# The last output tile in column parts of 384 and 128 instead of 256 and 256

## The chip, the core and the metric

The kernel runs on one core of a Trainium2 chip. The metric is device time in microseconds (us); the times below are from three timed runs and from one profiled execution. The engines are named as in the profile: PE is TensorE's matmuls, PEld its weight loads (which overlap the matmuls), DVE is VectorE, ACT is ScalarE, POOL is GpSimd, SP is SyncE, which issues the DMAs.

## The reference

Two attentions in a row, then a gated feed-forward layer:

```
p_packed = sm_attn(p, k, v)              # batch 8, heads 8, sequence 576, head 64; 32 packed queries
out = sm_attn(q, p_packed, p_packed)
x = out.transpose(0, 2, 1, 3).reshape(4608, 512)
a = x @ w_a                              # 512 x 1536
b = x @ w_b                              # 512 x 1536
result = (a * b) @ w_out                 # 1536 x 512, float32
```

## The kernel before, in words

The kernel walks over the 8 batches. For each it computes `h = a * b`, transposed, in 12 tiles of 128 rows of the hidden dimension (`NFT` is 12): `mm1` makes one of them in two matmul groups of 288 columns each (lines 356 to 381). Between these groups a written plan (`PLAN`, `emit`) places the attention steps of the next batch. Then the second product, `mm2_part` (line 387), makes the output for 128 tokens at a time: the 128x128 tile of `h` is the stationary operand and `w_out` streams past it.

To keep float32 accuracy every operand of the large products is split in a high and a low word (`_hi`, `_lo`, both of type float32r, kept as `h_hi`, `h_lo`, `wo_hi`, `wo_lo`), and a product is three matmuls: high with high, high with low, low with high. One output tile of 128 tokens therefore takes 12 x 3 = 36 matmuls, each with a weight load of its own of 128x128. Usually each streams all 512 columns of the output (`DO` is 512), and one ScalarE copy and one store follow (`mm2_out`).

The last tile of the last batch (`last`) is done differently. It is made in two column parts, one after the other, each in a PSUM buffer of its own from the pool `ps_m` (in the profile it is called `m`). ScalarE copies the first part to the output tile `ob` (in the profile `asb`), VectorE the second part; each part has a store of its own from SP's queue (line 403). So the copy and the store of the first part can run while TensorE works on the second part. After the second part nothing is left for TensorE, and what follows it is the program's tail: a VectorE copy, a DMA issue, the transfer, and the end.

Plain float32 matmuls, with operands that were not split, appear elsewhere in the kernel; `warm` (line 534), which streams 512 columns of a loaded tile nine times past the identity matrix, is one, and the transposes of lines 147 to 152 and 271 to 272 also stream float32 past the identity, by `nc.tensor.transpose`.

Of the kernel before, what the change touches and what calls it, by code (L numbers as in the profile page):

```python
# [19 lines left out]
def tile_packed_attn_gated_ffn(  # L20
# [20 lines left out]
    nc = tc.nc  # L41
# [3 lines left out]
    DO = out.shape[1]  # L45
    P = 128
# [44 lines left out]
    def bank_pair(s=False):  # L91
        return ps_s.tile([P, 2, 512], F32, name="s") if s else ps_m.tile([P, 2, 512], F32, name="m")
# [291 lines left out]
    def mm2_part(o, c0, fts, cols=slice(0, DO)):  # L384
        for ft in fts:
            for n, (ht, wt) in enumerate(((h_hi[ft], wo_hi[ft]), (h_hi[ft], wo_lo[ft]), (h_lo[ft], wo_hi[ft]))):
                nc.tensor.matmul(  # L387
                    out=o[:, cols], lhsT=ht[:, c0:c0 + P], rhs=wt[:, cols],
                    start=(ft == 0 and n == 0), stop=(ft == NFT - 1 and n == 2))

    def store(b, ob, c0, cols=slice(0, DO)):

        if b == 0:
            for i in range(2):
                store_first(ob, c0 // 64 + i, 64 * i)
            return
        t0 = b * S - 64 * (b % 2) + c0
        parts = [(t0 + 64 - S, 0, 64), (t0 + 64, 64, 64)] if c0 < 64 * (b % 2) else [(t0, 0, P)]
        if b == 1 and c0 == 0:
            store_first(ob, 0, 0)  # L400
            parts = parts[1:]
        for t, i, n in parts:
            nc.sync.dma_start(out=out[t:t + n, cols], in_=ob[i:i + n, cols])
# [10 lines left out]
    def out_tile(i):  # L414

        if i % 3 == 1:
            return sm.tile([P, DO], F32, name="wo_f32", bufs=1)
        return sm.tile([P, 2, HS], F32, name="asb").rearrange("p u t -> p (u t)")[:, 0:DO]
# [124 lines left out]
    for name in FIRST.split():  # L543
        what, i = name[0], int(name[1])
# [58 lines left out]
            mm2_out(b, o, c0, i)  # L603

    ob = out_tile(0)
    for i in range(2):
        o = bank_pair()[:, 0, :]
        cols = slice(i * DO // 2, (i + 1) * DO // 2)
        mm2_part(o, last, range(NFT), cols)
        copy = nc.vector.tensor_copy if i else nc.scalar.copy  # L610
        copy(out=ob[:, cols], in_=o[:, cols])
        store(B - 1, ob, last, cols)

# [29 lines left out]
```

## Time and profile before

| | |
|---|---|
| three timed runs, median (lowest, highest) | 732.89 us (731.39, 733.14) |
| profiled execution, its own time | 733.02 us |
| its span, first to last instruction | 731.2 us |
| TensorE matmul busy in the span | 98% |
| TensorE weight loads busy | 84% |
| VectorE, ScalarE, GpSimd busy | 41%, 39%, 29% |
| granted TensorE clock | mean 1.000 of full; 0.9 or more in all 40 slices |

The span is 1.8 us shorter than the profiled execution's time; what lies around it is not in the trace. A busy share says how long an engine had something in flight. Matmuls are pipelined, so a matmul's own duration is longer than the step from one to the next; what a matmul costs in a row of them is that step.

### The profile page before, as it was taken

How to read it: one execution, taken by the hardware profiler on the slowest of the kernel's cores; microseconds unless marked ns; L12 is line 12 of the kernel's file. 1: busy time of each engine (PE TensorE's matmuls, PEld its weight loads, DVE VectorE, ACT ScalarE, POOL GpSimd, SP SyncE). 2: the span in 40 equal slices, each digit the busy share in tenths (PEclk: the TensorE clock that was granted, in tenths of full speed). 3: DMA queues.
4: the chain of work that ended last, by engine and by line, in shares of the span. 5: the costliest groups of instructions: out<-in, count | busy, mean ns of one | idle time of the engine just before them, and what ended most of it. 6: DMA issues, size and time to landing. Idle time of an engine off the chain costs nothing.

```text
span 731.2 us, 14205 instructions
## 1 busy us (share of the span) xinstructions
PE 717.2 (98%) x6086; PEld 615.1 (84%) x6086; DVE 302.7 (41%) x487; ACT 281.7 (39%) x495; POOL 211.9 (29%) x154
## 2 busy tenths in 40 slices
PE   5899999999999999999999999999999999999998
PEld 4488878898888988898888988889888898898987
DVE  2788655456204562245602456045620546024100
ACT  2788743543115431354204442154311543135200
POOL 0486752334003340133202342033400334023300
PEclk9999999999999999999999999999999999999999
DMA  8999964350501505033320333215050100000011
GB/s 233 387 253 306 247 120 80 68 108 8 108 30 32 99 9 107 16 66 72 61 62 16 66 72 68 56 34 99 1 109 30 34 1 16 30 15 1 1 33 41
DMA packets 171007, 58.34 MB, mean 80 GB/s; under 512 B 140608, under 2 KB 158784, under 8 KB 170944
## 3 DMA queue, kind: packets, MB, share of 16 engines
q1 hardware_dynamic: 170944, 57.43, 32.2%
q8 instruction: 48, 0.79, 0.5%
q14 instruction: 15, 0.12, 0.0%
HBM read 47.97 MB, written 9.44 MB: 79 GB/s over the span
## 4 chain that ended last, share of the span: by engine, by line
PE 93%; DMA 3%; SPq 1%; ACT 1%; DVE 1%; issue 0%; DVEq 0%
PE m L361 42%; PE m L387 41%; PE x L343 4%; DMA raw<-in_moe_w_b_dram 2%; PE s L281 2%; PE m L343 1%; PE s L247 1%; DMA qn<-in_q_dram 1%; PE s L271 1%; PE s L297 1%; DVE w_ab L200 0%; PE x L236 0%; PE s L343 0%; PE m L297 0%; SPq L177 0%; SPq L169 0%
## 5 line engine op out<-in xcount | busy, mean ns | idle before, releaser
L387 PE MATMUL m<-wo,h_hi 128*128 128x512 f32 (+1 forms) x888 | 268.8, 385 | 0.0
L86 POOL TENSOR_TENSOR h_lo<-asb,h_hi 128x576 fp32r<-128x576 f32 x96 | 138.1, 1439 | 399.9 <-ACT h_hi L380 399.6
L376 DVE TENSOR_TENSOR asb<-m,asb 128x576 f32<-128x576 f32 x96 | 72.7, 757 | 307.0 <-PE m L361 302.3
L387 PEld LDWEIGHTS m<-wo,h_hi 128*128 128x128 f32 x888 | 164.2, 188 | 36.0 <-issue 3.4
L361 PE MATMUL m<-a_hi,ghi 128*128 128x288 f32 x768 | 169.5, 302 | 1.6 <-ACT ghi L349 1.5
L387 PE MATMUL m<-wo,h_lo 128*128 128x512 f32 (+1 forms) x444 | 170.2, 383 | 0.0
L361 PE MATMUL m<-a_lo,ghi 128*128 128x288 f32 x768 | 163.8, 295 | 0.3 <-DVE a_lo L86 0.3
L361 PEld LDWEIGHTS m<-a_hi,ghi 128*128 128x128 f32 x768 | 122.5, 188 | 20.7 <-issue 5.0
L361 PE MATMUL m<-a_hi,glo 128*128 128x288 f32 x768 | 133.7, 296 | 0.0
L361 PEld LDWEIGHTS m<-a_lo,ghi 128*128 128x128 f32 x768 | 123.9, 189 | 0.5 <-DVE a_lo L86 0.5
L380 ACT CAST h_hi<-asb 128x576 fp32r<-128x576 f32 x96 | 64.6, 673 | 143.5 <-DVE asb L376 143.5
L361 PEld LDWEIGHTS m<-a_hi,glo 128*128 128x128 f32 x768 | 112.9, 188 | 0.2 <-DVE glo L86 0.2
L387 PEld LDWEIGHTS m<-wo,h_lo 128*128 128x128 f32 x444 | 83.5, 188 | 16.5
L373 ACT COPY asb<-m 128x576 f32<-128x576 f32 x96 | 61.6, 642 | 30.9 <-PE m L361 24.0
L422 ACT COPY asb<-m 128x512 f32<-128x512 f32 x24 | 14.1, 587 | 133.3 <-PE m L387 132.2
L86 DVE TENSOR_TENSOR glo<-x,ghi 128x512 fp32r<-128x512 f32 x68 | 43.6, 682 | 4.5 <-ACT ghi L349 3.9
L343 PE MATMUL x<-w_ab,ppT 64*32 64x512 f32 x544 | 38.8, 591 | 0.2 <-DVE w_ab L200 0.2
L349 ACT CAST ghi<-x 128x512 fp32r<-128x512 f32 x68 | 36.6, 591 | 5.8 <-PE x L343 5.2
L119 DVE STREAM_TRANSPOSE xT<-nat 128x1152 f32<-128x1152 f32 x28 | 38.3, 1369 | 0.6 <-DMA nat<-in_k_dram 0.6
L422 ACT COPY wo_f<-m 128x512 f32<-128x512 f32 x11 | 6.5, 588 | 53.8 <-PE m L387 53.8
L189 ACT ACTIVATE raw<-raw 128x512 f32<-128x512 f32 x36 | 23.1, 681 | 1.9 <-DMA raw<-in_moe_w_a_dram 1.8
L315 POOL TENSOR_TENSOR t<-t,sum 128x576 f32<-128x576 f32 x14 | 16.5, 1179 | 24.9 <-DVE sum L314 24.9
(116 smaller groups left out, 474.3 us busy)
## 6 DMA issues: line engine op xcount, KB each, us to landing
nat<-in_k_dram SPq DMA_DIRECT2D x56, 144.0 KB
nat<-in_q_dram SPq DMA_DIRECT2D x56, 144.0 KB
vt<-in_v_dram SPq DMA_DIRECT2D x28, 256.0 KB
raw<-in_moe_w_a_dram SPq DMA_DIRECT2D x12, 512.0 KB
raw<-in_moe_w_b_dram SPq DMA_DIRECT2D x12, 512.0 KB
raw<-in_moe_w_out_dram SPq DMA_DIRECT2D x12, 512.0 KB
out_dram<-asb SPq DMA_DIRECT2D x17, 256.0 KB
out_dram<-wo_f SPq DMA_DIRECT2D x10, 256.0 KB
```

The source lines that it names most:

```text
L86: return eng.tensor_tensor(out=dst, in0=src, in1=hi.bitcast(F32), op=ALU.subtract)
L119: nc.vector.transpose(out=xT.rearrange("p h t -> p (h t)"), in_=t.rearrange("p h x d -> p (h x d)"))
L189: nc.scalar.activation(out=high, in_=high, func=AF.Prelu, scale=2.0 ** -112, alpha=-2.0 ** 32)
L315: eng.tensor_tensor(out=s2, in0=s2, in1=sum2.unsqueeze(2).broadcast_to([P, TU, J]), op=ALU.mult)
L343: nc.tensor.matmul(out=gps[e][J * r:J * r + J, 0:2 * P * n], lhsT=ppT[rows, 2 * (b % 2), r, :], rhs=w if n == 2 else w[:, fts[0] % 2], sta ...
L349: nc.scalar.copy(out=hi, in_=part)
L361: nc.tensor.matmul(out=ps[:, half, 0:HS], lhsT=gt[:, kt, ft % 4, cols], rhs=at[:, kt, HS * half:HS * half + HS], start=(n == 0 and kt == 0 ...
L373: nc.scalar.copy(out=asb, in_=pa[:, :, 0:HS])
L376: nc.vector.tensor_tensor(out=asb, in0=pb[:, :, 0:HS], in1=asb, op=ALU.mult)
L380: nc.scalar.copy(out=hh, in_=flat)
L387: nc.tensor.matmul(out=o[:, cols], lhsT=ht[:, c0:c0 + P], rhs=wt[:, cols], start=(ft == 0 and n == 0), stop=(ft == NFT - 1 and n == 2))
L422: nc.scalar.copy(out=ob, in_=o)
```

## The change

The two parts of the last tile are no longer 256 columns each. The first part has 384 columns, still copied by ScalarE; the second has 128, still copied by VectorE. The number of matmuls (36 in each part), their weight loads, their order, the copies and the stores are the same in number.

```diff
     ob = out_tile(0)
-    for i in range(2):
+    for cols, copy in ((slice(0, DO - P), nc.scalar.copy), (slice(DO - P, DO), nc.vector.tensor_copy)):
         o = bank_pair()[:, 0, :]
-        cols = slice(i * DO // 2, (i + 1) * DO // 2)
         mm2_part(o, last, range(NFT), cols)
-        copy = nc.vector.tensor_copy if i else nc.scalar.copy
         copy(out=ob[:, cols], in_=o[:, cols])
         store(B - 1, ob, last, cols)
```

On TensorE, where the first part of the last tile ends and the second begins, the order before is this (`m` is the PSUM buffer, `wo` the split `w_out`, `h_hi` and `h_lo` the split hidden tiles; the shape is what a matmul writes):

```order
L387 MATMUL m<-wo,h_lo_507 128x256
L387 MATMUL m<-wo,h_hi_508 128x256 x2
L387 MATMUL m<-wo,h_lo_509 128x256
L387 MATMUL m<-wo,h_hi_486 128x256 x2
L387 MATMUL m<-wo,h_lo_487 128x256
```

In the same place now:

```order
L387 MATMUL m<-wo,h_lo_507 128x384
L387 MATMUL m<-wo,h_hi_508 128x384 x2
L387 MATMUL m<-wo,h_lo_509 128x384
L387 MATMUL m<-wo,h_hi_486 128x128 x2
L387 MATMUL m<-wo,h_lo_487 128x128
```

No matmul moved: the same tiles follow one another, wider up to the middle and narrower from there. The end of SP's queue, which issues the stores, before (-) and now (+):

```order
 L403 DMA out_dram<-wo_f_7146 128x512
 L403 DMA out_dram<-asb 128x512 x2
-L403 DMA out_dram<-asb 128x256 x2
-L638 UNCONDITIONAL_BRANCH
+L403 DMA out_dram<-asb 128x384
+L403 DMA out_dram<-asb 128x128
+L636 UNCONDITIONAL_BRANCH
```

The two stores stand where they stood, with other widths.

## Rows read from the trace of the kernel before

**Rows 1.** The page: span, busy times, then the chain that ended last, by engine

```profile
span 731.2 us, 14205 instructions
PE 717.2 (98%) x6086; PEld 615.1 (84%) x6086; DVE 302.7 (41%) x487; ACT 281.7 (39%) x495; POOL 211.9 (29%) x154
PE 93%; DMA 3%; SPq 1%; ACT 1%; DVE 1%; issue 0%; DVEq 0%
```

**Rows 2.** The chain over 719 to 731.2 us: start, length, what

```profile
718.95 9.10 PE m L387 x74
728.04 0.04 DVEq L611
728.08 0.04 issue
728.12 0.42 DVE asb L611
```

**Rows 3.** Timeline of matmuls at L387: start, us until the last one's end

```profile
686.58 0.63 PE L387 MATMUL m<-wo,h_hi 128*128 128x512 f32 x2
...
719.24 0.40 PE L387 MATMUL m<-wo,h_hi 128*128 128x256 f32 x2
...
723.55 0.40 PE L387 MATMUL m<-wo,h_hi 128*128 128x256 f32 x2
...
727.75 0.28 PE L387 MATMUL m<-wo,h_lo 128*128 128x256 f32 x1
```

**Rows 4.** Groups by line and shape, 686.5 to 731.2 us: busy, mean ns

```profile
L387 PE MATMUL m<-wo,h_hi 128*128 128x512 f32 x96 | 29.6, 389 | 0.0
...
L387 PE MATMUL m<-wo,h_hi 128*128 128x256 f32 x48 | 8.7, 283 | 0.0
```

**Rows 5.** Four matmuls of 288 columns at 686 us: timeline, then their group

```profile
686.04 0.69 PE L361 MATMUL m<-a_hi,glo 128*128 128x288 f32 x4
L361 PE MATMUL m<-a_hi,glo 128*128 128x288 f32 x2 | 0.4, 293 | 0.0
```

**Rows 6.** Timeline at 723 us, a weight load and its matmul

```profile
723.31 0.19 PEld L387 LDWEIGHTS m<-wo,h_lo 128*128 128x128 f32 x1
723.43 0.28 PE L387 MATMUL m<-wo,h_lo 128*128 128x256 f32 x1
```

**Rows 7.** Weight loads of the whole span, by line and shape

```profile
L387 PEld LDWEIGHTS m<-wo,h_hi 128*128 128x128 f32 x888 | 164.2, 188 | 36.0 <-issue 3.4 <-ACT a_hi L319 0.4
...
L343 PEld LDWEIGHTS x<-w_ab,ppT 64*32 64x32 f32 x544 | 12.2, 106 | 4.6 <-PE m L534 1.0 <-issue 1.0 <-DVE w_ab L200 0.4
...
L271 PEld LDWEIGHTS s<-ident,t 128*128 128x128 f32 x56 | 6.9, 141 | 0.0
...
L272 PEld LDWEIGHTS s<-ident,t 128*64 128x64 f32 x14 | 1.6, 111 | 0.0
```

**Rows 8.** Transposes of L152: timeline of loads and matmuls, then the line's durations

```profile
21.56 0.57 PEld L152 LDWEIGHTS x<-ident,qn 32*128 32x128 f32 x8 [0.17 <-issue]
21.56 0.68 PE L152 MATMUL x<-ident,qn 32*128 32x32 f32 x8
L152 PEld LDWEIGHTS x<-ident,qn x8: 133/137/138, 21.6 to 22.0; 32*128 32x128 f32 x8
L152 PE MATMUL x<-ident,qn x8: 220/222/243, 21.6 to 22.0; 32*128 32x32 f32 x8
```

**Rows 9.** Plain float32 at L534: the line's count, then twelve in the timeline

```profile
L534 PE MATMUL m<-kn,ident x18: 592/592/697, 25.0 to 32.4; 128*128 128x512 f32 x18
27.64 5.31 PE L534 MATMUL m<-kn,ident 128*128 128x512 f32 x12
```

**Rows 10.** Copies: both parts of the last tile, and wider ones of either engine

```profile
L611 DVE COPY asb<-m 128x256 f32<-128x256 f32 x1 | 0.4, 425 | 40.5 <-PE m L387 40.5
L611 ACT COPY asb<-m 128x256 f32<-128x256 f32 x1 | 0.4, 373 | 3.7 <-PE m L387 3.7
L422 ACT COPY asb<-m 128x512 f32<-128x512 f32 x3 | 1.8, 588 | 21.8 <-PE m L387 21.8
L376 DVE TENSOR_TENSOR asb<-m,asb 128x576 f32<-128x576 f32 x1 | 0.8, 758 | 2.4 <-PE m L361 2.4
```

**Rows 11.** The last store: its issue, then DMA in 40 slices of 728 to 731.2 us

```profile
728.57 0.33 SPq L403 DMA_DIRECT2D out_dram<-asb  x1
DMA  0000000000000000028999510000000000000000
GB/s 0 0 0 0 0 0 0 0 0 0 0 0 0 0 0 0 0 90 294 346 358 333 192 26 0 0 0 0 0 0 0 0 0 0 0 0 0 0 0 0
```

**Rows 12.** The two halves and the tail, as windows: width, busy, PEclk, DMA, GB/s

```profile
719.24:723.55 4.31, 4.31 (x37) 4.31 (x36) 1.00 0.16 61
723.55:727.87 4.32, 4.32 (x38) 4.27 (x36) 1.00 0.11 34
727.87:731.20 3.33, 0.16 (x2) 0.00 (x0) 1.00 0.12 39
```

## The prediction

> **What bounds the kernel now.** I read the page first. Matmuls fill 98% of the span, and 93% of the chain that ended last is TensorE [rows 1]. So time is what TensorE's rows take, plus what follows the last of them. Then I took the chain over the last 12 us, to see who sets the end there: TensorE on line 387 without a break until 728.04 us, then the VectorE copy of the second part, 0.42 us [rows 2]. After it come the issue of the store, the transfer, and the end at 731.2 us. The first part's copy and store stand nowhere in this chain; they run under the second part. So two things count: the steps of 72 matmuls, and the tail behind the last one.
>
> Next the step from one matmul to the next, which is not the duration of one. 144 matmuls of 512 columns start between 686.58 and 719.24 us: 32.66 / 144 = 226.8 ns each. The 72 of 256 columns start from 719.24 to 727.75: 8.51 / 71 = 119.9 ns each [rows 3]. The difference over 256 more columns is 106.9 ns, or 0.418 ns a column, which is 2.4 GHz (the granted clock is 1.00 in these windows [rows 12]); about 13 ns do not depend on the width. The 288-column matmuls fit on the line: four take 0.69 us and one lasts about 0.29, so (0.69 - 0.29) / 3 = 133 ns [rows 5], and the line gives 119.9 + 32 x 0.418 = 133. Down to 256 columns, then, the columns alone set the step. The trace has no float32r matmul narrower than that.
>
> **The first part, 256 to 384 columns.** The line gives 119.9 + 128 x 0.418 = 173.3 ns a step. 36 of them: 36 x (173.3 - 119.9) = 1.92 us more. This term is an interpolation between measured widths, and I trust it to 0.1 us.
>
> **The second part, 256 to 128 columns.** If columns alone set the step here too, it is 119.9 - 53.5 = 66.4 ns, and what the first part loses comes back. The question is whether the weight loads let it. Each matmul has a 128x128 load of its own. At 256 columns the load for a matmul starts at 723.31 and its matmul at 723.43 [rows 6], about one step later, so a load has 120 ns and needs no more than that; with 66 ns it may need more than it has. The loads' durations (188 ns) contain a delay that overlaps with other loads, or a 120 ns step would not be possible. I take the delay out by comparing widths. A plain float32 load of 32 columns takes 106 ns, the 128-column load of line 387 takes 188: 82 / 96 = 0.854 ns a column, or 109 ns for 128 columns. The loads of the transposes are cheaper: 111 ns at 64 columns, 141 at 128 [rows 7], 0.469 ns a column, so 60 ns for 128.
>
> The second figure can be tried. The transposes of line 152 load 128 columns each and stream only 32, so that little but the load can set their step: eight loads in 0.57 us with 0.137 for the last make (0.57 - 0.137) / 7 = 62 ns, the matmuls (0.68 - 0.222) / 7 = 65 ns [rows 8]. The slope gave 60, so it forecasts a step bound by loads to 2 to 5 ns. For the loads of line 387 that makes 109 + 3 = **112 ns**, and I take it for the 128-column step. It is bounded by 66.4 ns below (columns alone) and 119.9 above, where loads of this very shape are seen to keep up.
>
> From the first start to the last there are 36 steps of the first part and 35 of the second, then the last matmul itself. That one lasts 283 ns at 256 columns and 389 at 512 [rows 4], so about 230 at 128. Before: 8.51 + 0.28 = 8.79 us. After: 36 x 173.3 + 35 x 112 + 230 = 6.24 + 3.92 + 0.23 = 10.39 us. TensorE loses **1.60 us**. By the bounds: 8.79 us at 66.4 ns (nothing lost), 10.67 at 119.9 (1.87 lost).
>
> Here a rule speaks against me. The Trainium skill, "TensorE: Matmul & The Clock Gate", section "Back-to-back issue gap", gives about 81 ns for a matmul of 128 columns in a sustained row of loads and matmuls. By its 81 ns the second part would be 35 x 31 = 1.1 us shorter than mine, and TensorE would lose an estimated 0.5 us. The same sentence has 131 ns for 512 columns, where this trace shows 227, so here the measured step decides for the wide matmul, and no run shows the narrow one yet.
>
> **The tail.** The last copy has half the columns. VectorE's copy of 256 takes 425 ns; between it and the 576-column pass of the same engine lies 333 ns for 320 columns, 1.04 ns each [rows 10]. 128 fewer save 0.13 us. The last store carries 64 KB instead of 128. Before, its data move in seven slices of 0.08 us, at most 0.56 us, from 729.36; its issue stood at 728.57 [rows 11]. The 0.8 us ahead of the data and the 1.3 us behind it are a wait that I leave as it is. Half of 0.56 is 0.28, if the transfer goes by bytes; if it goes by rows (128 in both cases) the gain is nothing. I take 0.2, since the rate near the middle of the transfer is flat, which is how bytes would look. Tail: **-0.33 us** (bounds -0.13 to -0.41).
>
> **What costs nothing.** ScalarE's first copy grows by 128 columns at (588 - 373) / 256 = 0.84 ns [rows 10], 0.11 us, and its store by 64 KB. Both lie under the second part, which at 112 ns a step is 36 x 112 = 4.0 us long. Copy (0.48 us), issue (0.33) and the 1.35 us from the issue to the end of the data that the last store shows [rows 11] make some 2.2 us, so they fit even under a part of 36 x 66.4 = 2.4 us. If that cover were gone, the price would be the rest of the first transfer ahead of the second, at most 0.3 us.
>
> **The sum.** 1.60 - 0.33 = +1.27 us on the profiled execution's 733.02 us (a span of 731.2 and 1.8 around it): 734.3. The median of the runs is 0.13 lower, so **734.2 us**, 0.17% slower. About 0.3%, 2.2 us, is what a measurement of this kernel can tell from no change, so this counts as the same.
>
> **The rivals.**
> - *The columns alone set the narrow step.* The loads are hidden at 66.4 ns as they are at 120; then TensorE loses nothing and the tail gains: 732.89 - 0.33 = 732.6 us. For it speaks the clean line from 512 down to 256; against it the slope of the load durations. By the 81 ns of the Trainium skill ("TensorE: Matmul & The Clock Gate", the section above) the time would lie between this and my sum, at an estimated 733.1 us.
> - *Narrow float32r goes at plain float32's pace.* The trace has float32r at 0.42 ns a column, but only at 256 and wider. Plain float32 is far slower: the nine matmuls of line 534 stand as 18 in the trace, each (5.31 - 0.592) / 11 = 429 ns after the one before [rows 9]. That is 858 ns for 512 columns, or 214.5 for 128. If the fast pace fails below some width, 35 x (214.5 - 112) = 3.6 us come on top of my sum, and it is 737.8 us: slower, by 0.7%. This decides from a step of about 140 ns on, where the sum passes 2.2 us. For it: every float32r matmul of the trace is at least 256 wide, so nothing contradicts it. Against it: plain float32 shows two loads and two matmuls for each, and no reason is seen why a narrower shape would add instructions.
> - *The loads do not get below 120 ns.* A variant of my case: 1.87 - 0.33, 734.4 us.
>
> **How the numbers follow.** I give 0.56 to the load-bound step (with the variant), 0.18 to the columns alone, 0.21 to the slow pace, 0.05 to anything else. The likeliest case by itself, with the bounds of its terms and the 1.75 us that the three runs are apart, is 733.2 to 735.2 us. Stopping there or at 732 below would leave the slow pace's 0.21 and more outside, so the range goes from 731.9 to 738.2. Slower by over 0.3%: the slow pace (0.21), a load-bound case that the scatter carries over 735.1 (0.05), something else (0.02): 0.28. Faster by over 0.3% needs under 730.7, which no case reaches without scatter: 0.03. The same: 0.69.
>
> **What would show it.** In the profile after: first-part matmuls 173 ns apart; second-part ones 112 ns apart, with a load busy throughout the second part, and a second part 4.0 us long instead of 4.3. The last copy would take 0.29 us, and from its end to the end of the span 2.5 us instead of 2.7. A second part of 2.4 us means the columns decide and I am wrong on the loads; one of 7 us or more means the slow pace. A first part that is not 6.2 us long would break the line itself.

## The result and the profile after

The changed kernel takes 734.14 us (median of 19 runs, 732.95 to 735.51), the kernel before 732.76 (19 runs, 731.39 to 733.74). The ratio is 1.0019, with a 95% interval from 1.0012 to 1.0025: slower by 0.9 to 1.8 us, 1.4 by the medians. That is a real loss, and within the 0.3% that I had called no change.

The profiled spans are 731.2 and 732.0 us, only 0.8 apart. Spans of single executions aren't the measure here: the last tile began at 719.24 us before and at 718.69 after, and the work ahead of it is the same in both. What the change did is read from that start on. Before, it is 731.2 - 719.24 = 11.96 us [rows 2, 3]; after, 732.0 - 718.69 = 13.31, that is **1.35 us more** (spans are given to 0.1 us), in agreement with the medians.

The chain over the end of the changed kernel (start, length, what; DVEq is VectorE's sequencer), against [rows 2]:

```profile
718.85 10.25 PE m L387 x72
729.10 0.03 DVEq L609
729.13 0.04 issue
729.18 0.29 DVE asb L609
```

The same members in the same order; TensorE's stretch is longer and the copy is 0.13 us shorter. Now the timeline of the changed kernel, at the start of each part and at the end (start, us until the last one's end), against [rows 3, 6, 11]:

```profile
718.69 0.51 PE L387 MATMUL m<-wo,h_hi 128*128 128x384 f32 x2
...
724.96 0.33 PE L387 MATMUL m<-wo,h_hi 128*128 128x128 f32 x2
725.07 0.19 PEld L387 LDWEIGHTS m<-wo,h_lo 128*128 128x128 f32 x1
725.12 0.27 PE L387 MATMUL m<-wo,h_lo 128*128 128x128 f32 x1
...
728.41 0.19 PEld L387 LDWEIGHTS m<-wo,h_lo 128*128 128x128 f32 x1
728.48 0.28 PE L387 MATMUL m<-wo,h_lo 128*128 128x128 f32 x1
728.53 0.30 PEld L387 LDWEIGHTS m<-wo,h_hi 128*128 128x128 f32 x2
728.59 0.39 PE L387 MATMUL m<-wo,h_hi 128*128 128x128 f32 x2
728.75 0.19 PEld L387 LDWEIGHTS m<-wo,h_lo 128*128 128x128 f32 x1
728.81 0.28 PE L387 MATMUL m<-wo,h_lo 128*128 128x128 f32 x1
729.18 0.29 DVE L609 COPY asb<-m 128x128 f32<-128x128 f32 x1 [42.12 <-PE m L387]
729.50 0.33 SPq L403 DMA_DIRECT2D out_dram<-asb  x1
```

The first part has steps of (724.96 - 718.69) / 36 = 174.2 ns, the second of (728.81 - 724.96) / 35 = **110.0 ns** on the mean. That mean holds a short first step: the first two narrow matmuls start 0.33 - 0.27 = 0.06 us apart. From the third on, at 725.12, 33 steps take 728.81 - 725.12 = 3.69 us, or **111.8 ns** each. The loads start every 0.11 us, at 728.41, 728.53 (two) and 728.75. A load now starts 0.06 us ahead of its matmul and not 0.12, as before the change [rows 6]. Before, it started together with the matmul ahead of its own, one step of 0.12 us before 723.43; now it starts 0.05 us behind that matmul (728.53 after 728.48). The loads no longer keep up with the matmuls.

The windows show the same (width, then matmul, weight load, VectorE, ScalarE and GpSimd busy, PEclk, DMA share, GB/s), against [rows 12]:

```profile
718.69:724.96 6.27, 6.27 (x38) 6.27 (x37) 0.00 (x0) 0.59 (x1) 0.00 (x0) 1.00 0.11 42
724.96:728.92 3.96, 3.96 (x37) 3.96 (x36) 0.00 (x0) 0.48 (x1) 0.00 (x0) 1.00 0.16 54
```

The second part is half as wide and only 8% shorter (3.96 us for 4.32), at the same granted clock. The load row by itself doesn't tell this: a load is "busy" all the time in the wide part as well. The starts do.

The last transfer, in 40 slices from 728.8 to 732 us, 0.08 us each, against [rows 11]:

```profile
DMA  0000000000000000000599300000000000000000
GB/s 0 0 0 0 0 0 0 0 0 0 0 0 0 0 0 0 0 0 0 154 294 263 103 6 0 0 0 0 0 0 0 0 0 0 0 0 0 0 0 0
```

Its data lie in five slices instead of seven. From the end of the copy (729.47 us) to the end of the span it is 2.53 us, against 2.66 before.

### The profile page after: what moved, and what is told of

Same layout as the page of the kernel before. It is cut to its first block, busy times and chain, and to the rows that moved or that the text cites. A ratio compares the mean times of both kernels' runs of the same rounds, so it can differ in the third digit from the quotient of the medians.

```text
span 732.0 us, 14205 instructions
## 1 busy us (share of the span) xinstructions
PE 719.0 (98%) x6086; PEld 616.7 (84%) x6086; DVE 302.7 (41%) x487; ACT 281.8 (38%) x495; POOL 212.4 (29%) x154
## 4 chain that ended last, share of the span: by engine, by line
PE 95%; DVE 1%; DMA 1%; ACT 1%; issue 0%; SPq 0%; DVEq 0%; ACTq 0%
PE m L361 42%; PE m L387 41%; PE x L343 4%; PE s L281 2%; PE m L343 1%; PE s L247 1%; PE s L271 1%; PE s L297 1%; DMA vt<-in_v_dram 1%; DMA kn<-in_k_dram 1%; PE x L236 0%; PE s L343 0%; PE x L147 0%; PE m L297 0%; PE m L147 0%
## 5 line engine op out<-in xcount | busy, mean ns | idle before, releaser
L387 PE MATMUL m<-wo,h_hi 128*128 128x512 f32 (+2 forms) x888 | 270.3, 386 | 0.0
L387 PEld LDWEIGHTS m<-wo,h_hi 128*128 128x128 f32 x888 | 164.7, 188 | 36.0 <-issue 3.4
L387 PE MATMUL m<-wo,h_lo 128*128 128x512 f32 (+2 forms) x444 | 170.8, 385 | 0.0
L387 PEld LDWEIGHTS m<-wo,h_lo 128*128 128x128 f32 x444 | 83.4, 188 | 16.6
```

What stands on the lines that cost most here:

```text
L387: nc.tensor.matmul(out=o[:, cols], lhsT=ht[:, c0:c0 + P], rhs=wt[:, cols], start=(ft == 0 and n == 0), stop=(ft == NFT - 1 and n == 2))
```

## The experiments

My theory was that the narrow step is the time of a weight load of 128x128, whatever the matmul's width. The rivals that were left after the trace: that a narrow float32r matmul streams at two cycles a column (128 x 2 / 2.4 GHz = 107 ns, nearly the same 110), and that the loss has to do with the place at the end of the program. The slow pace of plain float32 (214.5 ns) was already ruled out by the 110. The first step of the narrow part, 0.06 us, already speaks against two cycles a column, since it is too short for 107 ns.

**Other widths.** In two kernels the changed loop's `DO - P` became `DO - 64` and `DO - 192`:

```diff
-    for cols, copy in ((slice(0, DO - P), nc.scalar.copy), (slice(DO - P, DO), nc.vector.tensor_copy)):
+    for cols, copy in ((slice(0, DO - 64), nc.scalar.copy), (slice(DO - 64, DO), nc.vector.tensor_copy)):
```

> The last tile in 448 and 64 columns. If each matmul of the second part waits for its weight load (128x128, whatever the matmul's width), the narrow step stays at the 110 ns measured at 128 columns: second part 36 x 110 = 4.0 us, first part 36 x 200 = 7.2, together 2.5 us more than 256 and 256, and about 2.1 us slower than before with the shorter tail (734.9 from 732.8). If instead narrow float32r streams at two cycles a column, the step falls to some 55 ns (64 x 2 / 2.4): second part 2.0 us, together 0.5 us more. If the columns alone counted, about 40 ns and 1.4 us, together nothing more.

> The last tile in 320 and 192 columns. If the load sets the narrow step, it is 110 ns at 192 columns too (the line of the columns gives 93 there): second part 4.0 us, first part 36 x 147 = 5.3, together 0.6 us more than 256 and 256. If narrow float32r streams at two cycles a column, 160 ns and 5.8 us for the second part. If the columns alone set it, 93 ns and 3.4 us.

The timeline of the kernel with 448 and 64 columns, start of each part, third matmul of the second, and last matmul:

```profile
719.56 0.57 PE L387 MATMUL m<-wo,h_hi 128*128 128x448 f32 x2
...
726.85 0.30 PE L387 MATMUL m<-wo,h_hi 128*128 128x64 f32 x2
726.99 0.28 PE L387 MATMUL m<-wo,h_lo 128*128 128x64 f32 x1
...
730.67 0.28 PE L387 MATMUL m<-wo,h_lo 128*128 128x64 f32 x1
```

And of the one with 320 and 192:

```profile
718.34 0.45 PE L387 MATMUL m<-wo,h_hi 128*128 128x320 f32 x2
...
723.62 0.36 PE L387 MATMUL m<-wo,h_hi 128*128 128x192 f32 x2
723.82 0.28 PE L387 MATMUL m<-wo,h_lo 128*128 128x192 f32 x1
...
727.51 0.28 PE L387 MATMUL m<-wo,h_lo 128*128 128x192 f32 x1
```

The steps are (730.67 - 726.85) / 35 = 109.1 ns at 64 columns and (727.51 - 723.62) / 35 = 111.1 at 192. At 64, 128 and 192 columns the mean step is the same to 2%. The small drift with the width comes from the start of the part: from the third matmul on, the steps are (730.67 - 726.99) / 33 = 111.5 ns and (727.51 - 723.82) / 33 = 111.8, against 111.8 at 128, so no dependence on the width is seen. Two cycles a column would have been 53 and 160 ns, and is out, as are the columns alone. In time the 448 and 64 kernel is at a ratio of 1.004 to the kernel before (1.0026 to 1.0055), 735.49 us; that is 1.9 to 4.0 us more, 3.2 by the medians of 5 and 8 runs, where 2.1 were expected. From the start of the last tile to the end its trace has 733.7 - 719.56 = 14.14 us, 2.18 more than before. The 320 and 192 kernel ran once, at 732.62 us; in its trace TensorE takes (727.51 + 0.28) - 718.34 = 9.45 us for the last tile instead of 8.79, 0.66 more, where 0.6 was expected.

**Half the load, the same columns.** The matmuls of the second part take 64 tokens as weights, and so write 64 rows:

```diff
-                    out=o[:, cols], lhsT=ht[:, c0:c0 + P], rhs=wt[:, cols],
+                    out=o[0:m, cols], lhsT=ht[:, c0:c0 + m], rhs=wt[:, cols],
...
+        m = P if cols.start == 0 else P // 2
```

> 384 and 128 columns, but the second part loads only 64 of the tile's 128 tokens as weights, so it leaves out 64 tokens by 128 columns of the output. If the load sets the narrow step, half the load (about 55 ns) is hidden under the 66 ns of the columns: the step falls from 110 to about 66 ns, the second part from 4.0 to 2.4 us. If the 110 ns come from the 128 streamed columns themselves, nothing changes: 110 ns.

Its timeline, start of the second part and end:

```profile
725.46 0.28 PE L387 MATMUL m<-wo,h_hi 128*64 128x128 f32 x2
...
727.50 0.14 PEld L387 LDWEIGHTS m<-wo,h_lo 128*64 128x64 f32 x1
727.56 0.22 PE L387 MATMUL m<-wo,h_lo 128*64 128x128 f32 x1
```

The step falls to (727.56 - 725.46) / 35 = 60.0 ns with the same 128 columns streamed: with half the weights to load the narrow matmuls run at nearly the speed of their columns (53.3 ns). The edit also halves the rows that a matmul writes, but what is written changes with the columns too, and the step was the same at 64, 128 and 192 of them. A fixed cost of each load and matmul pair is out as well, since there are as many pairs as before. Together the two experiments leave the load. I had expected 66, since I took the 13 ns beside the columns for the matmul's own; 60.0 is 6.7 above the columns. A further run looked at that. This kernel ran once, at 732.83 us. Of the 35 x 50 = 1.75 us that its steps save against the change, 0.35 goes to a longer tail: from the last matmul's start to the end it has 731.1 - 727.56 = 3.54 us against 3.19, and the reason was not looked for.

**Half the load at 256 columns.** The same edit with parts of 256 and 256.

> 256 and 256 columns, with weights of 64 tokens in the second part (64 tokens by 256 columns are left out). With 128 columns this gave a step of 60.0 ns, 7 ns above the columns' 53.3, where the wide matmuls stand 13 above. If the 13 ns are the matmul's own, the step stays at 120. If half of them belong to the load of 128 columns, it is about 113.

```profile
724.10 0.40 PE L387 MATMUL m<-wo,h_hi 128*64 128x256 f32 x2
...
728.08 0.28 PE L387 MATMUL m<-wo,h_lo 128*64 128x256 f32 x1
```

(728.08 - 724.10) / 35 = 113.7 ns, 7.0 above the columns' 106.7. So about half of the 13 ns goes with half the load, or with half the rows written, which this edit changes too. The 113 was the second of the two expectations. This run is the cleaner evidence: at 128 columns half a load, some 55 ns, lies as near to the 60.0 as the columns do.

**The cost repeated elsewhere.** The four full tiles of the last batch, ahead of the last one, are made in two passes as well, into the same buffer:

```diff
-            for f in range(f0, NFT, 3):
...
+            if b == B - 1:
+                for cols in (slice(0, DO - P), slice(DO - P, DO)):
+                    mm2_part(o, c0, range(NFT), cols)
+            else:
+                for f in range(f0, NFT, 3):
...
```

> The four full tiles of the last batch are also made in parts of 384 and 128 columns, in one PSUM buffer and with one copy and one store each as before; on top of the change. Each tile should take 36 x (174.2 + 110.0) = 10.23 us instead of 36 x 226.8 = 8.16, so 8.3 us more for four by the load's step: 742.4 us from 734.1, or 1.3% above the kernel before. If the loss of the change came from its place at the end (the tail, the last buffers), and not from the steps, these four cost only the 13 ns a matmul that does not depend on the width, 1.9 us.

It takes 741.98 us, where 742.4 was expected, at a ratio of 1.013 to the kernel before (1.0115 to 1.0145); beside the 732.26 us of the kernel before on that chip that is 9.7 us more, 8.3 of it beyond the change's 1.4. A window over the first of these tiles (columns as above):

```profile
685.67:695.90 10.23, 10.23 (x75) 10.23 (x73) 0.76 (x1) 0.68 (x1) 1.47 (x2) 1.00 0.01 2
```

10.23 us instead of 36 x 226.8 = 8.16. The loss is in the steps and not in the place at the end: it is paid wherever the narrow pass stands.

**The tail by itself.** Parts of 256 and 256 as before, with the second copy and store cut to 128 columns:

```diff
-        copy(out=ob[:, cols], in_=o[:, cols])
-        store(B - 1, ob, last, cols)
+        kept = cols if i == 0 else slice(DO - P, DO)
+        copy(out=ob[:, kept], in_=o[:, kept])
+        store(B - 1, ob, last, kept)
```

> 256 and 256 columns as before, but the second part's copy and store take only its last 128 columns, so 128 columns of the last 128 tokens are left out. This is the tail of the change without its matmuls. The steps stay at 120 ns. The copy should take 0.29 us instead of 0.425. By the prediction the transfer gains 0.2 us more; by the trace of the change the stretch from the copy's end to the end of the span was 2.53 us against 2.66, so 0.13. Last matmul's start to the end of the span: 3.2 us, against 3.45 before.

The timeline at its end:

```profile
726.32 0.28 PE L387 MATMUL m<-wo,h_lo 128*128 128x256 f32 x1
726.69 0.29 DVE L612 COPY asb<-m 128x128 f32<-128x128 f32 x1 [40.52 <-PE m L387]
```

From the last matmul's start to the end of the span: 729.5 - 726.32 = 3.18 us, as in the changed kernel (732.0 - 728.81 = 3.19), against 731.2 - 727.75 = 3.45 before. So the change's tail gains 0.26 to 0.27 us, whatever TensorE does. One run took 731.31 us; the scatter of single runs is larger than the gain, and the reading is the trace's.

**No split at all.** If a narrow part costs, so might any split: two parts pay the 13 ns of 36 matmuls once more, 0.46 us. Two kernels make the last tile in one pass and copy and store its halves behind it; the second issues the first half's store from ScalarE's queue.

```diff
-    for i in range(2):
-        o = bank_pair()[:, 0, :]
+    o = bank_pair()[:, 0, :]
+    mm2_part(o, last, range(NFT))
+    for i in range(2):
         cols = slice(i * DO // 2, (i + 1) * DO // 2)
-        mm2_part(o, last, range(NFT), cols)
```

> The last tile in one part of 512 columns, then both copies (256 columns each, ScalarE and VectorE side by side) and both stores behind it. TensorE: 35 x 226.8 + 389 = 8.33 us instead of 8.79, 0.46 less, if a matmul costs 13 ns beside its columns. The copies lie side by side, 0.43 us. The second store is issued behind the first on one queue, 0.33 us later, and 128 KB more have to move: 0.3 to 0.6 us more. So 0.1 us less to 0.15 more in all: no change that can be measured. If splitting the tile paid by hiding the first copy and store, this would be 0.5 us slower or more.

> As whole, with the first half's store issued by ScalarE's queue, beside SP's. The issue is not serial, so 0.3 us less behind the copies than whole: 0.2 to 0.4 us less than the kernel before. That is 0.05%, below what timing tells; the trace from the last matmul's start to the end of the span should show it.

The first is at 1.0005 (0.9996 to 1.0014) of the kernel before, the second at 1.0003 (0.9992 to 1.0013): no difference, and no version that beats the kernel before. The first agrees with what was expected of it, though not for the reason given. The timeline of the first, at the start of the last tile and from its last matmul:

```profile
717.45 0.62 PE L387 MATMUL m<-wo,h_hi 128*128 128x512 f32 x2
...
725.38 0.39 PE L387 MATMUL m<-wo,h_lo 128*128 128x512 f32 x1
725.85 0.37 ACT L611 COPY asb<-m 128x256 f32<-128x256 f32 x1 [7.57 <-PE m L387]
726.25 0.85 SPq L403 DMA_DIRECT2D out_dram<-asb  x2
726.31 0.42 DVE L611 COPY asb<-m 128x256 f32<-128x256 f32 x1 [40.50 <-ACT asb L611]
```

The two copies do not lie side by side. VectorE's waited for ScalarE's (its releaser is ACT at L611), and starts 0.46 us behind it; both read one PSUM buffer and write one output tile, and which of the two puts them in order was not tried. From the first matmul's start to the last one's it is 725.38 - 717.45 = 7.93 us, 0.58 less than the 8.51 before; from there to the end it is 729.4 - 725.38 = 4.02 us, 0.57 more than the 3.45 before. The longer tail uses up what TensorE saves. The second kernel, from its last matmul:

```profile
726.06 0.39 PE L387 MATMUL m<-wo,h_lo 128*128 128x512 f32 x1
...
726.93 0.38 ACTq L613 DMA_DIRECT2D out_dram<-asb  x1
726.99 0.42 DVE L611 COPY asb<-m 128x256 f32<-128x256 f32 x1 [40.50 <-ACT asb L611]
727.44 0.33 SPq L613 DMA_DIRECT2D out_dram<-asb  x1
```

It has 730.1 - 726.06 = 4.04 us: its expected gain of 0.2 to 0.4 us did not come, since the copies stand in a row there too. In neither kernel does the second half's issue wait for the first's: the first issue is over (726.25 + 0.33, and 727.31) before VectorE's copy ends (726.73, and 727.41). Whether side-by-side copies would gain was not tried.

## Why the prediction was right

- **What bounds the end.** TensorE's 72 steps and the tail, nothing else; the chain after shows the same members. Right.
- **The first part**, 173.3 ns a step by interpolation: 174.2 measured.
- **The second part**, 112 ns from the slope of the load durations over their widths: 110.0 measured on the mean, 111.8 from the third matmul on. The 3 ns that were added to the slope's 109 belong there; the mean is lower because the part starts with a short step. The rival by the columns alone would have been 66.4 and the slow pace 214.5; both are out, and the experiments show that it is the load and not the stream that takes the 110 ns.
- **How good that slope is.** That it came within a nanosecond is luck in part. It took its two widths from two lines of the program and two types, plain float32 at 32 columns and float32r at 128. The half loads give the slope again on line 387 itself. The first two rows below are from the kernel with half loads at 128 columns, and 188 and 136 are the mean ns of one load; the third is from the one at 256, with the shortest, median and longest load (the shortest are the half loads):

```profile
L387 PEld LDWEIGHTS m<-wo,h_hi 128*128 128x128 f32 x30 | 5.5, 188 | 0.3
...
L387 PEld LDWEIGHTS m<-wo,h_hi 128*64 128x64 f32 x24 | 2.2, 136 | 0.0
...
L387 PEld LDWEIGHTS m<-wo,h_hi x56: 134/187/192, 716.8 to 727.9; 128*128 128x128 f32 x32, 128*64 128x64 f32 x24
```

The first kernel has (188 - 136) / 64 = 0.81 ns a column, 104 ns for 128; the second (192 - 134) / 64 = 0.91, or 116. So the method gives the cost to some 6 ns, enough to tell it from 66.4 and from 214.5.

- **The two rules of the Trainium skill.** In its page "TensorE: Matmul & The Clock Gate", section "Back-to-back issue gap", the Trainium skill has 81 ns for such a pair at 128 columns; that doesn't hold for this form, where 110.0 was measured. The section "LDWEIGHTS (loading the stationary operand)" of the same page of the Trainium skill gives a load's time as its columns over 1.2 GHz, an estimated 107 ns for 128 columns; the mean step is 3% above that and the steady one 5%. The transposes of line 152 do not agree with it: they load 128 columns too, in steps of 62 ns [rows 8].
- **"The columns alone" down to 256.** The prediction's reading of the wide matmuls was not quite right. At 256 columns half the load brought the step from 119.9 to 113.7 ns, so part of the 13 ns beside the columns was never the matmul's own. The forecast does not change by it, since every load in it has 128 columns.
- **TensorE's sum.** +1.60 us forecast from the first start to the last matmul's end; (728.81 + 0.28) - 718.69 = 10.40 us after against 8.79 before, +1.61 measured. That it agrees to 0.01 is luck: three small errors cancel in it. The second part's steps took 0.07 us less than forecast, the first part's 0.03 more, and the last matmul lasted some 280 ns and not 230, 0.05 more. In the second part all matmuls but the first last 272 to 278 ns at 64, 128 and 192 columns; the first, which had its load early, lasted 193, 221 and 251 ns.
- **The tail.** -0.33 forecast, -0.26 measured. The copy gave exactly its 0.13. The transfer is the term that was mis-sized: 0.13 instead of 0.2. Its data began 0.8 us after the issue and ended 1.3 us before the end of the span both times, and lay in five slices (the last nearly empty) instead of seven: half the bytes took some 0.16 us less, not half of 0.56. The peak rate was lower too, 294 GB/s against 358 [rows 11].
- **What costs nothing.** ScalarE's first copy ran from 725.20 to 725.68 us, and ended 3.8 us ahead of the last issue. Right. The prediction's sum for this cover counts the issue twice, since the 1.35 us begin with it; it is some 1.8 us and not 2.2, and nothing hangs on that.
- **The whole.** +1.27 on the profile's time forecast, +1.35 measured from the last tile's start, +1.4 between the medians.

The prediction's reading that this counts as the same holds by its own bound of 0.3%, but that bound is not what a measurement can tell: with 19 runs on either side the loss is told from nothing.

## What to carry to other kernels

Splitting a matmul's columns costs the 13 ns of every added matmul, and much more below the width at which its weight load is just hidden. For these float32r loads of 128x128 with their 111.8 ns an estimate of that width is (111.8 - 13) / 0.418 = about 236 columns; between 192 and 256 no width was run. Such a floor can be read before it is met, from loads of two widths: the slope of their durations, not the durations, is what one costs in a row of them, here to some 6 ns. A shorter tail by a narrower last part is weighed against all the steps of that part: here 0.26 us bought for 1.61.

## What was not expected of the hardware

The constant beside a matmul's columns is not all the matmul's own: it was about 13 ns with 128 weight columns and 7.0 with 64, at 256 streamed columns in both cases. At 128 streamed columns it was 6.7 with 64, though there the half load may bound the step instead. The two widths make an estimated 0.1 ns a weight column. Whether it goes with the load or with the rows written, and what it consists of, was not tested.
